# The scale of v of two batches as a sum on ScalarE instead of a maximum on VectorE, with a new table of turns

## The chip, the cores and the metric

One core of one Trainium2 chip. The time is that of the device for one execution, in microseconds. One execution of the kernel before was also recorded by the hardware profiler; all rows here are from it.

## The reference

Attention with random features (8 batches, 8 heads, 576 tokens, 64 wide, 128 features), then a feed-forward layer over the 4608 tokens, all in float32:

```python
def phi(x):                                   # x is q or k, scaled by 64 ** -0.25
    proj = np.einsum('bhsd,md->bhsm', x, omega)
    h = proj - np.sum(x * x, axis=-1, keepdims=True) / 2.0
    h = h - np.max(h, axis=-1, keepdims=True)
    return np.exp(h) / np.sqrt(m)
q_p, k_p = phi(q_s), phi(k_s)
kv = np.einsum('bhsm,bhsd->bhmd', k_p, v)
z = np.sum(k_p, axis=2)
num = np.einsum('bhsm,bhmd->bhsd', q_p, kv)
den = np.einsum('bhsm,bhm->bhs', q_p, z)[..., None] + 1e-06
x = (num / den) transposed to (4608, 512)
h = x @ w_in                                  # 512 to 2048
out = np.maximum(0.01 * h, h) @ w_out         # 2048 to 512
```

w_in and w_out come as 64-bit floats (8 MB each) and are turned into 32-bit words on the chip.

## The kernel before

Most matmuls run in float16, three for each product: a number is split into a high and a low half, and high by high, high by low and low by high are added. The first key batches (0 and 1) and the first query block run in float32 instead (`Whole`). Splitting is done by `high` (L412, L414 on VectorE, L416 on ScalarE) and `low_` (L422, VectorE or GpSimd).

The work goes over nine blocks of 512 tokens. For each pair of heads (hp) of a block, q is projected (L721 in float32, L657 in float16), its features are made on VectorE and ScalarE, turned (L912, or a transposing DMA), multiplied with kv (the numerators, L941 or L934 to L936) and divided (L951 to L954), which gives x. x is split and turned by a transposing DMA (L869) and goes through the feed-forward layer: up products (L1307 for the first three blocks, L1217 with seven products of half blocks after that), down products (L1331, at the end L1141). The low parts of the rows between them are L422 into `fix_big`, sums of half blocks are L983.

Keys come by batch: projection, features, and the sums with v (L824). Before that v of a batch gets a scale (`values`): a power of two made from one number for each partition. For that number VectorE reduces each of two halves of v (128x1280) to the largest absolute value (L759) and takes the larger of both (L762); `power_of_two` spreads it by a matmul (L447) and makes the power on VectorE (L451 to L456). v times that power is L416 on ScalarE. What the power was is taken out again in `row_scale`. The weights are read in eight pieces each (L516, L518), turned into float32 words (L531 to L554), summed for a scale (L544) and split (L578, L416, L422).

Every operation is recorded with its possible engines, a cost and its buffers. `Plan.order` then places them one after the other, by a model of the engines: the ready operation with the smallest priority goes first, and it takes the engine that would finish it first. Three tables change that order by the operation's number: TURNS moves its priority, HELD lets a matmul of the feed-forward layer wait or go earlier, ONLY names its engine. Tile buffers of a kind are handed out in the same order, so the table also sets which buffer an operation gets. Where the model sees TensorE idle for over 0.4 us, `between` puts throwaway matmuls (`busy`, L1382) that keep its clock up. All DMAs are issued by one queue (SP) in the order found.

The lines of the order's rule that the tables enter:

```python
o.prio -= 1e-4 * (o.tail - TURNS.get(o.number, 0.0))
t += SLACK["PE"] * o.slack + HELD.get(o.number, 0.0)
e = min([ONLY[o.number]] if o.number in ONLY else o.ways, key=...)
```

Of the kernel before, what the change touches and what calls it, by code (L numbers as in the profile page):

```python
# [1442 lines left out]
```

## Time and profile before

| | |
|---|---|
| median of 3 runs | 930.81 us (929.64 to 931.83) |
| profiled execution | 930.82 us, span 929.0 us |
| TensorE busy (PE) | 910.3 us, 98% |
| VectorE busy (DVE) | 737.3 us, 79% |
| ScalarE busy (ACT) | 561.1 us, 60% |
| GpSimd busy (POOL) | 374.4 us, 40% |
| mean granted clock of TensorE | 0.996 |

The span runs from the first to the last instruction. Busy times are sums of instructions; a busy TensorE includes the throwaway matmuls.

### The profile page before, as it was taken

What the parts mean: (1) busy time and instruction counts of PE and PEld (TensorE: products, weight loads), DVE (VectorE), ACT (ScalarE), POOL (GpSimd) and SP (SyncE); (2) the same over time, 40 slices, a digit from 0 to 9 for tenths busy, and PEclk for the clock granted to TensorE, in tenths of its full rate; (3) what the DMA queues carried; (4) which work ended last, traced back from release to release, by engine and by line L of the source; (5) the groups of instructions that cost most, each with busy time, mean ns of one, the idle gap of its engine ahead of it and who ended that gap; (6) DMA issues with size and microseconds to landing.
All of it is one profiled execution on the core that took longest, in us unless ns stands there. A gap on an engine that the chain in (4) does not pass through costs nothing.

```text
span 929.0 us, 20977 instructions
## 1 busy us (share of the span) xinstructions
PE 910.3 (98%) x8519; PEld 607.6 (65%) x8519; DVE 737.3 (79%) x1311; ACT 561.1 (60%) x867; POOL 374.4 (40%) x343
## 2 busy tenths in 40 slices
PE   7989999999999999999999999999999999999997
PEld 6887465545555445588558855885588558846886
DVE  7889988898888967888887889787889762476874
ACT  5888586756765556568647765575467545522551
POOL 2334443566615544236222532250226233664541
PEclk9999999999999999999999999999999999999999
DMA  9684538756477379678767876794688767721301
GB/s 355 256 273 133 129 102 170 177 134 171 77 187 149 84 183 232 154 192 206 188 126 178 223 161 147 185 210 91 136 197 206 140 126 176 165 58 60 100 1 46
DMA packets 257729, 145.92 MB, mean 157 GB/s; under 512 B 191328, under 2 KB 237152, under 8 KB 256608
## 3 DMA queue, kind: packets, MB, share of 16 engines
q1 hardware_dynamic: 257632, 144.58, 63.7%
q8 instruction: 66, 1.08, 0.5%
q14 instruction: 31, 0.25, 0.1%
HBM read 81.36 MB, written 16.78 MB: 106 GB/s over the span
## 4 chain that ended last, share of the span: by engine, by line
PE 84%; DMA 6%; DVE 4%; ACT 3%; POOL 1%; issue 1%; SPq 0%; DVEq 0%; ACTq 0%
PE fixps_ffn L1331 32%; PE fixps_ffn L1217 20%; PE fixps_ffn L1307 10%; PE attps_pj L657 5%; PE lateps_ffn L1331 3%; DMA fix_big<-w_in 3%; PE lateps_ffn L1217 3%; PE lateps_ffn L1141 2%; PE attps_mi L934 1%; DMA att_t<-att_z 1%; DMA att_qp<-att_ph 1%; POOL fix_wt L551 1%; PE fixps_ffn L1141 1%; PE attps_mi L824 1%; PE attps_mi L936 1%
## 5 line engine op out<-in xcount | busy, mean ns | idle before, releaser
L1331 PE MATMUL fixps_ffn<-fix_wt,fix_big 128*128 128x512 f16 x1392 | 313.2, 379 | 0.0
L1331 PEld LDWEIGHTS <-fix_big 128*128 128x128 f16 x1536 | 145.6, 98 | 166.6
L422 POOL TENSOR_TENSOR fix_big<-fix_row,fix_big 128x512 f16<-128x512 f32 x118 | 154.7, 1321 | 179.9 <-ACT fix_big L416 148.1
L1217 PEld LDWEIGHTS <-fix_wt 128*128 128x128 f16 x2016 | 194.9, 98 | 24.5
L1217 PE MATMUL fixps_ffn<-fix_xt,fix_wt 128*128 128x256 f16 x1800 | 204.3, 273 | 0.0
L1307 PE MATMUL fixps_ffn<-fix_xt,fix_wt 128*128 128x512 f16 x576 | 129.3, 379 | 0.0
L1307 PEld LDWEIGHTS <-fix_wt 128*128 128x128 f16 x576 | 54.7, 98 | 62.5
L676 ACT ACTIVATE att_p<-att_p,shift 128x1024 f32<-128x1024 f32 (+1 forms) x68 | 69.8, 1029 | 34.9 <-DVE att_p L673 34.7
L664 DVE TENSOR_REDUCE att_st<-attps_pj 128x8 f32<-128x1024 f32 x68 | 72.6, 1075 | 17.3 <-PE attps_pj L657 17.2
L422 DVE TENSOR_TENSOR att_ph<-att_p,att_ph 128x1024 f16<-128x1024 f32 x56 | 75.4, 1353 | 6.8 <-ACT att_ph L416 6.5
L416 ACT ACTIVATE fix_big<-fix_row 128x512 f16<-128x512 f32 x124 | 75.4, 624 | 8.4 <-DVE fix_row L983 5.3
L673 DVE SCALAR_TENSOR_TENSOR att_p<-attps_pj,att_sc,att_st 128x1024 f32<-128x1024 f32 x68 | 76.7, 1132 | 0.2
L1232 DVE TENSOR_TENSOR fix_row<-fix_row,fixps_ffn 128x512 f32<-128x512 f32 x64 | 43.8, 684 | 38.8 <-PE fixps_ffn L1217 20.7
L422 POOL TENSOR_TENSOR fix_xn<-fix_x,fix_xn 128x512 f16<-128x512 f32 (+1 forms) x28 | 31.8, 1134 | 90.4 <-ACT fix_xn L416 84.7
L617 ACT ACTIVATE att_z<-att_nat 128x512 f32<-128x512 f32 (+1 forms) x56 | 36.2, 647 | 43.6 <-DMA att_t<-att_z 35.0
L1240 ACT ACTIVATE fix_row<-fix_row 128x512 f32<-128x512 f32 x70 | 43.5, 624 | 18.3 <-DVE fix_row L1232 17.8
L657 PEld LDWEIGHTS <-att_t 64*128 64x128 f16 x1416 | 39.7, 94 | 19.1 <-issue 15.2
L416 ACT ACTIVATE att_ph<-att_p 128x1024 f16<-128x1024 f32 x48 | 50.4, 1049 | 3.0 <-PE attps_mi L824 1.6
L657 PE MATMUL attps_pj<-om,att_t 64*128 64x128 f16 x1416 | 50.3, 217 | 1.8 <-DMA att_t<-att_z 1.6
L416 ACT ACTIVATE fix_row<-fixps_ffn 128x512 f32<-128x512 f32 x47 | 27.8, 594 | 32.8 <-PE fixps_ffn L1217 29.3
L641 DVE SCALAR_TENSOR_TENSOR att_z<-att_nat,att_sc,att_z 128x512 f16<-128x512 f32 (+1 forms) x52 | 45.8, 881 | 2.2 <-ACT att_z L416 1.9
L416 ACT ACTIVATE fix_row<-fixps_ffn,fix_s 128x512 f32<-128x512 f32 x26 | 17.8, 683 | 49.3 <-PE fixps_ffn L1331 49.2
(202 smaller groups left out, 1645.2 us busy)
## 6 DMA issues: line engine op xcount, KB each, us to landing
fix_wt<-w1s SPq DMA_DIRECT2D x38, 512.0 KB, 4.9
fix_wt<-w1s SPq DMA_DIRECT2D x38, 384.0 KB, 3.7
att_v<-vn SPq DMA_DIRECT2D x16, 650.0 KB, 5.8
out<-fix_row SPq DMA_DIRECT2D x34, 256.0 KB, 2.3
fix_big<-w_in SPq DMA_DIRECT2D x8, 1024.0 KB, 11.2
fix_big<-w_out SPq DMA_DIRECT2D x8, 1024.0 KB, 6.5
att_nat<-qn SPq DMA_DIRECT2D x32, 256.0 KB, 3.0
w1s<-fix_y SPq DMA_DIRECT2D x32, 128.0 KB, 2.4
```

The source lines that it names most:

```text
L416: ("ACT", act(n, int(pointer)), lambda: nc.scalar.activation(dst(), src(), AF.Copy, scale=1.0 if scale is None else value()), False),
L422: return ways([(e, c, lambda g=g: g.tensor_tensor(dst(), a(), b(), op=ALU.subtract), True) for e, c, g in (("POOL", pool_(n), nc.gpsimd), ...
L641: op("DVE", stt(n) + 0.15, lambda: nc.vector.scalar_tensor_tensor(zl(), heads(), up(), zh(), op0=ALU.mult, op1=ALU.subtract), port=True, r ...
L657: nc.tensor.matmul(at(pj)[:, 512 * h + c * M:512 * h + (c + 1) * M], at(self.t)[r, 2 * (c0 + c) + x, :], om[r, w, :], start=(x + w == 0), ...
L664: op("DVE", dve(n * M), lambda: nc.vector.tensor_reduce(row(0), pv(), axis=AX.X, op=ALU.max), r=[pj], w=[st], prio=prio)
L673: op("DVE", dve(n * M), lambda: nc.vector.scalar_tensor_tensor(p(), pv(), down(), row(2).rearrange("p (g o) -> p g o", o=1).broadcast_to([ ...
L676: op("ACT", act(n * M, 1), lambda: nc.scalar.activation(flat(p()), flat(p()), AF.Exp, bias=shift), w=[p32], r=["ones"], prio=prio)
L1217: nc.tensor.matmul(o, unit(at(wb[c]), u)[:, wp, P * a:P * a + P], mixes[j, c][n][1](xp), start=(first and a == 0 and i == 0), stop=(a == 1 ...
L1232: op("DVE", dve(512), lambda: nc.vector.tensor_tensor(at(g), at(g), at(b), op=ALU.add), r=[b], w=[g], prio=top - 1.0)
L1240: op("ACT", act(512), lambda: nc.scalar.activation(at(g), at(src), AF.Prelu, scale=H_DOWN_D if finish else H_DOWN_S, alpha=0.01), r=[src], ...
L1307: nc.tensor.matmul(at(ph), wk[wp][:, c:c + P], xt[:, xp, :], start=(i == 0), stop=(i == 3 * KT - 1))
L1331: nc.tensor.matmul(at(po), part(f, gp)[:, t * P:(t + 1) * P], wf[wp], start=(n == 0 and f % 4 == 0 and gp == wp), stop=(n == 3 and f % 4 = ...
```

## The change

For batches 0 and 1 the two reduces of v on VectorE are replaced by two passes of ScalarE: the absolute value of a quarter of v, whose sum over the row (1280 numbers) the engine accumulates into the same two numbers. The values themselves go into a spare buffer of the kind z, which is not read. Everything behind it (the larger of the two, the power of two) is as it was; the power is another one and is taken out again like the first. Batches 2 to 7 keep the maximum. The three tables are replaced by new ones: TURNS has 2083 entries (214 before), HELD 220 (22) and ONLY 260 (109).

```diff
+V_ACT = (0, 1)
 READ_SUM = 0.2
 TURNS = {
-    17: -8162.408562, 19: 107.254804, 21: -271.649377, 24: -147.714435, 36: -50.284217, 51: 163.113317,
...
+    4: -247.528796, 5: -9365.02752, 6: -16958.431273, 7: -36741.43905, 8: -36505.728899, 9: -44080.908038,
...
         mx2, mx = one(f"mx2_v{b}", [P, 2]), one(f"mx_v{b}", [P, 1])
         for j in range(2):
-            op("DVE", dve(half * D), lambda j=j: nc.vector.tensor_reduce(mx2[:, j:j + 1],
-               at(raw)[:, j * half:(j + 1) * half, :D], axis=AX.XY, op=ALU.max, apply_absolute_value=True), r=[(raw, j)],
-               w=[f"mx2_v{b}{j}"], prio=prio)
+            x = lambda j=j: at(raw)[:, j * half:(j + 1) * half, :D]
+            if b not in V_ACT:
+                op("DVE", dve(half * D), lambda j=j, x=x: nc.vector.tensor_reduce(mx2[:, j:j + 1], x(), axis=AX.XY, op=ALU.max,
+                   apply_absolute_value=True), r=[(raw, j)], w=[f"mx2_v{b}{j}"], prio=prio)
+                continue
+            spare = buf("z")
+            op("ACT", act(half * D) + 0.25, lambda j=j, x=x, spare=spare: nc.scalar.activation(
+                at(spare).rearrange("p a b -> p (a b)").bitcast(BF16)[:, :half * D].rearrange("p (g d) -> p g d", d=D), x(),
+                AF.Abs, scale=0.25, accum_out=mx2[:, j:j + 1]), r=[(raw, j)], w=[spare, f"mx2_v{b}{j}"], prio=prio)
```

With the longer tables the code's lines move: L1307 is L1698 in the changed kernel, L954 is L1345, L516 is L901, L700 is L1085, L755 is L1140, L531 is L916, L416 is L801, L728 is L1113, L1382 is L1773.

The start of the program on the DMA queue. Before (kT, qT are keys and queries, omT is omega, vn is v, eye the identity):

```order
L700 DMA att_nat_159<-kT 128x640
L467 DMA fix_xt_98<-omT 128x256
L468 DMA ident<-eye 128x128
L516 DMA fix_big_88<-w_in 128x2048
L516 DMA fix_big_89<-w_in 128x2048
L516 DMA fix_big_90<-w_in 128x2048
L516 DMA fix_big_91<-w_in 128x2048
L755 DMA att_v_175<-vn 128x1300 x2
L700 DMA att_nat_160<-kT 128x640
L755 DMA att_v_176<-vn 128x1300 x2
```

Of the change:

```order
L901 DMA fix_big_88<-w_in 128x2048
L901 DMA fix_big_89<-w_in 128x2048
L901 DMA fix_big_90<-w_in 128x2048
L901 DMA fix_big_91<-w_in 128x2048
L1140 DMA att_v_175<-vn 128x1300
L1085 DMA att_nat_159<-kT 128x640
L1085 DMA att_nat_160<-kT 128x640
L1140 DMA att_v_175<-vn 128x1300
L852 DMA fix_xt_98<-omT 128x256
L853 DMA ident<-eye 128x128
```

Four pieces of w_in have moved ahead of keys, omega and identity.

VectorE where the scale of batch 0 is made (mx_v_128 holds the two numbers of its halves, mx_v_129 the larger). Before:

```order
L759 TENSOR_REDUCE mx_v_128<-att_v_175 128x1 x2
L536 SCALAR_TENSOR_TENSOR fix_wt_69<-fix_big_90,fix_wt_69 128x1024
L536 SCALAR_TENSOR_TENSOR fix_wt_71<-fix_big_91,fix_wt_71 128x1024
L762 TENSOR_REDUCE mx_v_129<-mx_v_128 128x1
L728 TENSOR_REDUCE att_st_179<-attps_pj_201 128x8
L451 TENSOR_REDUCE pow_v_130<-attps_mi_203 128x1
```

Of the change:

```order
L921 SCALAR_TENSOR_TENSOR fix_wt_71<-fix_big_91,fix_wt_71 128x1024
L864 TENSOR_SCALAR fix_xt_98<-fix_xt_98 128x256
L865 TENSOR_REDUCE mx_om<-fix_xt_98 128x1
L1153 TENSOR_REDUCE mx_v_129<-mx_v_128 128x1
L836 TENSOR_REDUCE pow_om<-attps_mi_203 128x1
```

The reduces of v are gone from there, and the scale of omega, which had been made before the first piece of w_in, is now made behind the fourth.

ScalarE at the end of the first query block (mx_v_135 belongs to batch 1, fix_xn to the split of x). Of the change:

```order
L801 ACTIVATE fix_xn_86<-fix_x_84 128x512
L934 ACTIVATE fix_wt_79<-fix_big_88 128x1024
L1150 ACTIVATE att_z_161,mx_v_135<-att_v_176 128x1280
L1150 ACTIVATE att_z_162,mx_v_135<-att_v_176 128x1280
L1086 ACTIVATE att_z_161<-att_nat_159 128x512
L1086 ACTIVATE att_z_162<-att_nat_160 128x512
L801 ACTIVATE fix_kv_82<-fix_kv_81 128x260
L801 ACTIVATE fix_xn_87<-fix_x_84 128x512
```

The two passes over v of batch 1 stand between the copies of x of the third and of the fourth pair of heads, where there was nothing of v.

## Rows read from the trace of the kernel before

**Rows 1.** Busy time of each engine in two stretches, cut at the start of the first up product (PE, PEld, DVE, ACT, POOL: us busy and instructions; then granted clock, share of the DMA engines, GB/s).

```profile
0.00:89.32 89.32, 79.14 (x848) 70.66 (x849) 76.11 (x124) 67.63 (x83) 27.31 (x22) 0.96 0.71 251
89.32:929.00 839.68, 831.12 (x7674) 536.95 (x7671) 661.19 (x1188) 493.43 (x786) 347.06 (x322) 1.00 0.64 147
```

**Rows 2.** Timeline of TensorE: the last numerators of the first query block, throwaway matmuls, the first up product, and the last matmuls of the program (start us, us, engine, line, operation).

```profile
81.23 1.10 PE L941 MATMUL attps_mi<-fix_kv,att_qp 128*128 128x65 f32 x8
85.06 4.42 PE L1382 MATMUL fixps_ffn<-ident 128*128 128x256 f16 x39
89.32 2.75 PE L1307 MATMUL fixps_ffn<-fix_xt,fix_wt 128*128 128x512 f16 x12
...
917.73 6.71 PE L1141 MATMUL lateps_ffn<-fix_wt,fix_big 128*128 128x256 f16 x60
```

**Rows 3.** What TensorE waited for, longest in total first (us in total, times, longest).

```profile
...
PE fixps_ffn L1141 <- DVE fix_big L422: 1.6, 1, 1.6
PE attps_pj L657 <- DMA att_t<-att_z: 1.6, 1, 1.6
```

**Rows 4.** Busy time of each engine from the start to the end of the eighth L954, in three stretches, and their sum (columns as in rows 1).

```profile
0.00:9.60 9.60, 4.56 (x38) 4.33 (x40) 3.62 (x17) 2.45 (x3) 0.20 (x4) 1.00 0.77 268
9.60:45.00 35.40, 33.57 (x399) 29.87 (x397) 32.73 (x43) 27.41 (x32) 10.66 (x10) 1.00 0.78 311
45.00:83.67 38.67, 35.47 (x362) 31.73 (x362) 34.14 (x56) 32.11 (x44) 13.23 (x7) 0.91 0.65 210
sum 83.67, PE 73.60 PEld 65.93 DVE 70.50 ACT 61.98 POOL 24.09; mean PE 24.53 PEld 21.98 DVE 23.50 ACT 20.66 POOL 8.03
```

**Rows 5.** Groups of VectorE instructions by line and shape (count, busy us and mean ns of one, then idle time before them).

```profile
L759 DVE TENSOR_REDUCE mx_v<-att_v 128x1 f32<-128x1280 f32 x16 | 23.5, 1479 | 1.7 <-DMA att_v<-vn 1.7
L422 DVE TENSOR_TENSOR fix_big<-fix_row,fix_big 128x512 f16<-128x512 f32 x23 | 20.1, 876 | 1.5 <-ACT fix_big L416 1.4
L730 DVE TENSOR_TENSOR att_ph<-attps_pj,att_st 128x1024 f32<-128x1024 f32 x12 | 14.6, 1218 | 0.8 <-DMA att_qp<-att_ph 0.8
L728 DVE TENSOR_REDUCE att_st<-attps_pj 128x8 f32<-128x1024 f32 x12 | 14.6, 1214 | 1.8 <-PE attps_pj L721 1.8
L533 DVE TENSOR_SCALAR fix_wt<-fix_wt 128x1024 uint32<-128x1024 uint32 x16 | 13.5, 851 | 2.5 <-ACT fix_wt L531 1.5 <-issue 0.9
L412 DVE CAST att_ph<-att_p 128x1024 f16<-128x1024 f32 x8 | 6.4, 806 | 0.2 <-ACT att_p L676 0.2
L412 DVE CAST fix_xn<-fix_y 128x512 f16<-128x512 f32 x4 | 2.1, 513 | 0.0
L414 DVE TENSOR_SCALAR fix_row<-fixps_ffn,fix_s 128x512 f32<-128x512 f32 x2 | 1.5, 752 | 3.5 <-PE fixps_ffn L1331 3.5
L422 DVE TENSOR_TENSOR fix_kv<-fix_kv,fix_kv 128x260 f16<-128x260 f32 x2 | 0.8, 416 | 0.0
```

**Rows 6.** Timeline of VectorE: the division behind a numerator, with the idle time before it and what ended that (in brackets), and the eighth L954.

```profile
73.67 0.16 DVE L951 TENSOR_SCALAR att_r<-attps_mi 128x4 f32<-128x4 f32 x1 [1.15 <-PE attps_mi L941]
...
83.24 0.42 DVE L954 TENSOR_TENSOR fix_x<-attps_mi,att_r 128x256 f32<-128x256 f32 x1
```

**Rows 7.** Timelines of the queue (SPq), ScalarE and GpSimd: issues at the start, the first instructions that waited for pieces of w_in and for the second block of keys, and the high and low part of the fourth pair of heads.

```profile
0.74 0.41 SPq L700 DMA_DIRECT2D att_nat<-kT  x1
...
2.13 1.85 SPq L516 DMA_DIRECT2D fix_big<-w_in  x4
...
9.17 1.13 ACT L531 ACTIVATE fix_wt<-fix_big 128x1024 f32<-128x1024 f32 x1 [4.50 <-DMA fix_big<-w_in]
...
16.59 1.18 ACT L531 ACTIVATE fix_wt<-fix_big 128x1024 f32<-128x1024 f32 x1 [0.30 <-DMA fix_big<-w_in]
...
21.38 0.74 ACT L701 ACTIVATE att_z<-att_nat 128x640 f32<-128x640 f32 x1 [0.92 <-DMA att_nat<-kT]
...
84.50 0.62 ACT L416 ACTIVATE fix_xn<-fix_x 128x512 f16<-128x512 f32 x1
...
85.20 1.21 POOL L422 TENSOR_TENSOR fix_xn<-fix_x,fix_xn 128x512 f16<-128x512 f32 x1 [3.23 <-ACT fix_xn L416]
```

**Rows 8.** Groups of ScalarE instructions by line and shape, and busy time of each engine from 70 to 85 us (columns as in rows 5 and 1).

```profile
L416 ACT ACTIVATE att_v<-att_v,pow_v 128x1280 f32<-128x1280 f32 x16 | 21.3, 1350 | 0.0
L617 ACT ACTIVATION_READ_ACCUMULATOR att_z<-att_nat 128x1 f32 x56 | 10.5, 188 | 0.0
L701 ACT ACT_TABLE_LOAD x1 | 1.3, 1283 | 0.7 <-PEq L1436 0.7
...
70.00:85.00 15.00, 14.29 (x138) 12.39 (x137) 13.74 (x22) 10.85 (x17) 4.37 (x2) 0.91 0.36 104
```

**Rows 9.** Timeline of TensorE: the first and the last of the sixteen rows of four matmuls of two projections in f32 (L721) that stand back to back.

```profile
59.01 0.49 PE L721 MATMUL attps_pj<-fix_xt,att_nat 64*128 64x128 f32 x4
...
62.46 0.39 PE L721 MATMUL attps_pj<-fix_xt,att_z 64*128 64x128 f32 x4
```

**Rows 10.** Busy time of each engine from 590 to 690 us (columns as in rows 1).

```profile
590.00:690.00 100.00, 99.56 (x1004) 70.40 (x1003) 81.78 (x156) 62.43 (x103) 25.91 (x26) 1.00 0.71 159
```

**Rows 11.** Timelines of VectorE and of GpSimd near the end: two sums of half blocks (L983) on VectorE, and what GpSimd ran at the time of the first.

```profile
902.26 1.65 DVE L983 TENSOR_TENSOR fix_row<-fix_row,fix_row 128x512 f32<-128x512 f32 x1
...
909.23 0.68 DVE L983 TENSOR_TENSOR late_row<-late_row,fix_row 128x512 f32<-128x512 f32 x1
...
902.09 2.83 POOL L422 TENSOR_TENSOR fix_big<-fix_row,fix_big 128x512 f16<-128x512 f32 x2 [3.98 <-DVE fix_big L412]
```

More of the change, by code (lines that the diff above doesn't have):

```diff
@@ L113 @@
-    1365: "DVE", 1420: "DVE", 1485: "DVE", 1593: "DVE", 1597: "DVE", 1612: "DVE", 1646: "DVE", 1649: "DVE",
-    1656: "DVE", 1664: "DVE", 1672: "DVE", 1693: "DVE", 1699: "DVE", 1741: "DVE", 1916: "DVE", 1926: "DVE",
-    1927: "DVE", 1934: "DVE", 1953: "DVE", 1956: "DVE", 1957: "DVE", 1972: "DVE", 1992: "DVE", 2008: "DVE",
-    2011: "DVE", 2025: "DVE", 2044: "DVE", 2048: "DVE", 2053: "DVE", 2174: "DVE", 2184: "DVE", 2188: "DVE",
-    2195: "DVE", 2198: "DVE", 2204: "DVE", 2226: "DVE", 2258: "DVE", 2304: "DVE", 2307: "DVE", 2311: "DVE",
@@ L118 @@
-    2314: "DVE", 2365: "DVE", 2375: "DVE", 2470: "DVE", 2537: "DVE", 2540: "DVE", 2541: "DVE", 2547: "DVE",
-    2569: "DVE", 2627: "DVE", 2629: "DVE", 2737: "DVE", 2740: "DVE", 2752: "DVE", 2759: "DVE", 2765: "DVE",
-    2824: "DVE", 2884: "DVE", 2897: "DVE", 2913: "DVE", 2966: "DVE", 2976: "POOL", 2977: "DVE", 3007: "POOL",
-    3014: "POOL", 3027: "DVE", 3030: "ACT", 3036: "POOL", 3046: "DVE", 3059: "POOL", 3082: "DVE", 3092: "DVE",
-    3095: "POOL", 3113: "DVE",
+    77: "DVE", 102: "DVE", 210: "DVE", 313: "DVE", 314: "DVE", 325: "DVE", 333: "DVE", 334: "DVE", 342: "DVE",
@@ new lines @@
+    346: "POOL", 350: "DVE", 357: "DVE", 376: "DVE", 460: "DVE", 465: "DVE", 479: "DVE", 483: "DVE", 486: "DVE",
+    490: "DVE", 492: "DVE", 497: "DVE", 499: "DVE", 502: "DVE", 503: "DVE", 505: "DVE", 538: "DVE", 564: "DVE",
+    565: "DVE", 661: "DVE", 688: "DVE", 712: "DVE", 717: "DVE", 723: "DVE", 762: "DVE", 802: "ACT", 898: "DVE",
+    929: "DVE", 953: "DVE", 961: "DVE", 965: "DVE", 976: "DVE", 977: "DVE", 984: "DVE", 985: "DVE", 1001: "DVE",
+    1004: "DVE", 1005: "DVE", 1009: "DVE", 1019: "ACT", 1025: "DVE", 1084: "DVE", 1134: "DVE", 1136: "DVE",
@@ new lines @@
+    1138: "DVE", 1139: "DVE", 1140: "DVE", 1141: "DVE", 1143: "DVE", 1204: "DVE", 1253: "DVE", 1276: "DVE",
+    1306: "DVE", 1315: "DVE", 1330: "DVE", 1340: "DVE", 1353: "DVE", 1359: "DVE", 1371: "DVE", 1485: "DVE",
+    1492: "DVE", 1495: "DVE", 1596: "DVE", 1597: "DVE", 1600: "DVE", 1631: "DVE", 1640: "DVE", 1659: "DVE",
+    1665: "DVE", 1670: "DVE", 1679: "DVE", 1694: "DVE", 1701: "DVE", 1707: "DVE", 1711: "DVE", 1712: "DVE",
+    1785: "DVE", 1843: "DVE", 1869: "DVE", 1877: "DVE", 1880: "DVE", 1930: "DVE", 1933: "DVE", 1934: "DVE",
@@ new lines @@
+    1935: "DVE", 1936: "DVE", 1940: "DVE", 1948: "DVE", 1950: "DVE", 1966: "DVE", 1972: "DVE", 1976: "DVE",
+    1982: "DVE", 1996: "DVE", 2000: "DVE", 2001: "DVE", 2006: "DVE", 2025: "DVE", 2034: "DVE", 2037: "DVE",
+    2044: "DVE", 2047: "DVE", 2052: "DVE", 2053: "DVE", 2087: "DVE", 2098: "DVE", 2120: "DVE", 2128: "DVE",
+    2152: "DVE", 2187: "DVE", 2188: "DVE", 2190: "DVE", 2191: "DVE", 2192: "DVE", 2193: "DVE", 2194: "DVE",
+    2204: "DVE", 2212: "DVE", 2241: "DVE", 2290: "DVE", 2293: "DVE", 2300: "DVE", 2303: "DVE", 2304: "DVE",
@@ new lines @@
+    2340: "DVE", 2359: "DVE", 2370: "DVE", 2372: "DVE", 2379: "DVE", 2393: "DVE", 2407: "DVE", 2408: "DVE",
+    2412: "POOL", 2416: "ACT", 2429: "DVE", 2435: "DVE", 2441: "DVE", 2455: "DVE", 2477: "DVE", 2516: "DVE",
+    2534: "DVE", 2535: "DVE", 2537: "DVE", 2538: "DVE", 2547: "DVE", 2580: "DVE", 2594: "ACT", 2626: "DVE",
+    2629: "ACT", 2630: "DVE", 2633: "DVE", 2634: "DVE", 2635: "DVE", 2636: "DVE", 2637: "DVE", 2639: "ACT",
+    2640: "DVE", 2643: "DVE", 2648: "POOL", 2656: "DVE", 2666: "DVE", 2667: "DVE", 2671: "ACT", 2672: "POOL",
@@ new lines @@
+    2676: "ACT", 2677: "DVE", 2682: "DVE", 2685: "DVE", 2686: "POOL", 2692: "DVE", 2695: "DVE", 2696: "POOL",
+    2705: "ACT", 2706: "DVE", 2708: "DVE", 2714: "ACT", 2715: "DVE", 2730: "POOL", 2735: "POOL", 2740: "ACT",
+    2743: "DVE", 2747: "DVE", 2753: "DVE", 2759: "DVE", 2771: "DVE", 2813: "ACT", 2823: "ACT", 2824: "POOL",
+    2826: "DVE", 2827: "DVE", 2829: "DVE", 2830: "POOL", 2831: "DVE", 2833: "DVE", 2834: "DVE", 2865: "DVE",
+    2873: "DVE", 2891: "DVE", 2893: "DVE", 2894: "DVE", 2896: "DVE", 2897: "DVE", 2928: "DVE", 2930: "DVE",
@@ new lines @@
+    2938: "DVE", 2959: "DVE", 2964: "POOL", 2967: "POOL", 2969: "DVE", 2982: "DVE", 2983: "POOL", 2998: "DVE",
+    3002: "DVE", 3006: "POOL", 3009: "POOL", 3014: "POOL", 3016: "ACT", 3017: "DVE", 3024: "ACT", 3035: "ACT",
+    3036: "POOL", 3046: "ACT", 3047: "POOL", 3049: "ACT", 3050: "POOL", 3055: "POOL", 3062: "DVE", 3064: "DVE",
+    3065: "POOL", 3067: "POOL", 3077: "DVE", 3091: "DVE", 3093: "POOL", 3095: "DVE", 3096: "DVE", 3102: "POOL",
+    3103: "DVE", 3106: "POOL", 3108: "POOL", 3110: "POOL", 3112: "POOL", 3114: "DVE", 3116: "POOL", 3117: "DVE",
@@ L123 @@
+    3124: "DVE", 3133: "DVE", 3140: "DVE", 3141: "DVE", 3149: "DVE", 3156: "DVE", 3164: "DVE",
 }
```

4 lines of the change are left out of this document (removed), and 444 rows, old and new, of tables (HELD, TURNS).

## The prediction

> **What bounds the kernel now.** The two stretches of [rows 1] come first, cut at the start of the first up product (L1307) at 89.32 us [rows 2]. From there to the end TensorE is busy for 831.1 of 839.7 us, so that part is the matmuls themselves. In the 89.3 us ahead of it TensorE only serves a chain that others pace. The order of the changed program has the same matmuls on both sides of the first up product; only the throwaway matmuls (L1382, all ahead of it) go from 233 to 205. So the time is the start of the first up product, plus 831.1 us that neither order changes, plus whatever TensorE waits behind it, now 8.6 us. The waits of TensorE [rows 3] list two longer ones there, 1.6 us for the transposed z (at about 110 us) and 1.6 us for VectorE's low part of a half block (at 908.8 us); 4.6 us more are the drain from the last matmul, 924.4, to the end of the span [rows 2].
>
> The stretch ahead of the first up product is paced by VectorE. Its last instruction that matters there is the eighth L954 (the second half of x of the fourth pair of heads), which ends at 83.67 us [rows 6]; up to there it works 70.5 us and idles 13.2 [rows 4]: 6.0 in the first 9.6 us, 2.7 to 45 and 4.5 to 83.7. One wait of the last part is 1.15 us for TensorE's numerators [rows 6]. From 83.67 it takes 5.65 us more: high part on ScalarE, low part on GpSimd, transposing DMA [rows 2, 7].
>
> **VectorE's list.** I count what stands in VectorE's queue ahead of the eighth L954, 115 instructions before and 114 now. Gone are the four reduces of batches 0 and 1 (but the two of batch 2 now stand ahead of it, so a net two), two L728, one L730 and one L533. At the durations of [rows 5]: 2 x 1.48 + 2 x 1.21 + 1.22 + 0.85 = 7.45 us. New are a cast of a weight piece (nearest row 0.81), a cast of x (0.51), and two small ones of kv (0.42 each; one of them has the row, the other I take alike): 2.16 us; one more maximum of two numbers I leave out. Net -5.3, so 65.2 us of work.
>
> **What ScalarE pays.** An Abs pass over 128x1280 with a sum is not in the trace. The nearest row is the L416 copy of v of the same shape, 1.35 us, plus the read of the accumulator, 0.19 us [rows 8]: 1.54 us each, 6.2 us in all. Free is not excluded by any row for the first two (ScalarE waits there for transfers, [rows 7]); the upper bound is the sum. The order has one table load before and one now, so none is added to the 1.28 us of [rows 8]. The passes of batch 0 take the place of waiting. Those of batch 1 stand ahead of the copy of x of the fourth pair; ScalarE is idle for 4.15 us between 70 and 85 us [rows 8], which covers them; without that cover they cost 3.1 us there.
>
> **The transfers move.** The queue now begins with four pieces of w_in, and the keys, omega and the identity, which were first, come behind them. The first row of the queue issues at 0.74 us; the first piece of w_in was issued at 2.13 and had landed at 9.17 [rows 7], 7.0 us later, so it should now land at 7.8 and VectorE start on it at 8.9, after ScalarE's 1.13. The fourth piece had landed at 16.59, 7.4 us behind the first, so it is there at 15.2. Omega stands behind 6.3 MB; the second block of keys stood behind 6.4 MB and landed at 21.4, so omega is there at about 21.2, where before its chain was over by 8.3. VectorE's idle time now: 8.2 us to the first piece; to about 25.7 us 1.5 for the pace of the pieces, 1.9 for omega, 0.9 inside the omega chain (as its wait for L447 now) and 0.4 for the first projection; then 2.0 to 45 us (2.7 from 9.6 to 45 now, nearly all of it behind 20). Behind 45 us it was 4.5. In the new order the weights are converted earlier and the queries' projections stand ahead of the sums, so I take 1.5, with 0 and 4.5 as ends. Sum 16.4 us, 3.2 more than now.
>
> So the eighth L954 ends at 65.2 + 16.4 = 81.6 us, 2.1 us earlier. Behind it the data need the high part, 0.62, the low part, 1.21, and 2.9 from its end at 86.4 to the up product at 89.3 [rows 2, 7]: 4.7 us. TensorE still has 64 projections of batch 1 (3.85 us from 59.01 to 62.85, [rows 9]), 22 throwaway matmuls at 0.109 (39 in 4.24, [rows 2]) and one group of sums (0.2) between the last numerator and the up product, 6.45 us, counted from 1.3 us ahead of the end of L954: 5.1. So the first up product starts at 86.7, **-2.6 us**.
>
> **Behind the first up product.** The projection that waited 1.6 us for its transposed z had seven up products (2.6 us each) between the start and itself; now it has eight. I take half the wait, -0.8, with 0 and -1.6 as ends. The wait at 908.8 I leave as it is (0 to -1.65). The new table also moves work onto VectorE for the rest of the run: 48 more L422, 36 more casts (L412), 16 more L414, four fewer L983; at 0.88, 0.51 and 0.75 us [rows 5], and 0.9 for the last (between the 0.68 and 1.65 of [rows 11]), that is 42 + 18 + 12 - 4, less 5.9 for the four reduces: +62 us. GpSimd has 44 instructions fewer, ScalarE 43. VectorE goes from 737 to 799 us, of some 926. The cover is its idle time, 178 us of the 839.7 [rows 1]. The densest added stretch has ten more L422 and ten more L412, 13.9 us on the 81.8 of 100 between 590 and 690 us [rows 10]: 96, still under. I price it at nothing, with +7 us as the other end (third rival).
>
> **Sum.** 930.82 (this execution, span 929.0 and 1.82 around it; the median of the runs shown is 930.81) - 2.6 - 0.8 = **927.4 us**. No other time is taken from the table.
>
> **One row against a rule.** Beside GpSimd's additions of 1.6 us the same L983 takes VectorE 1.65 us, and 0.68 alone [rows 11]: about 1 us lost for each overlap. The Trainium skill (SBUF — State Buffer, Who interferes with whom) says that a VectorE instruction with both inputs in SBUF and a GpSimd instruction that reads SBUF exclude each other, and that the later one blocks until the first is done. The trace agrees. By that rule the 48 moved L422 are exposed to lock-outs that they did not have on GpSimd, and at 1 us each that would be another 48 us, 847 of some 926; but GpSimd also has 44 instructions fewer to lock with. The sum goes by the mean rows, in which the overlaps of now are contained.
>
> **Rivals.**
> *The front costs more than it gives* (0.17). Keys and omega come 15 us later. If the transfers of the first two query blocks, behind 12.2 MB, land at 38 us and not 35, the chain of the queries starts 3 us later, and VectorE's idle time behind 45 us stays at 4.5. For it: behind 6.4 MB the second keys landed at 21.4 [rows 7], so 12.2 MB at the same pace are there at 36 and not earlier. Against it: VectorE has conversions to do until then. First up product at 89 to 90 us, total 930.
>
> *All of it is gained* (0.16). VectorE never idles behind 45 us (-1.5), and both waits of TensorE go (-0.8 and -1.65 more): 923.5. For it: the list alone is 5 us shorter, and the new order has 28 throwaway matmuls fewer, 3.0 us of TensorE. Against it: three engines must arrive together at the numerators, as they did not in [rows 6].
>
> *VectorE locks out in the down products* (0.15), the other side. The moved L422 sit between a finished half block and the products that read it. One place like that waits 1.65 us now [rows 3, 11]. If the added instructions make such a wait at each of four more places in the last six blocks, that is +6.6, total 934 (927.4 + 6.6). It decides from the second such wait on, which eats the 3.4.
>
> That the change doesn't do what it says I exclude: the order has no reduce for batches 0 and 1.
>
> **How the numbers follow.** The likeliest case (0.49) has its own range of 924.5 to 930 from the ends of the idle time and the two waits; I give 0.40 of it to faster and 0.09 to same. A measurement tells about 0.2%, 1.9 us, from no change. The front rival gives 0.13 to same, 0.04 to slower; the full gain 0.16 to faster; the lock-out 0.14 to slower, 0.01 to same; 0.03 is left for what I don't see (0.01 each). That makes 0.57, 0.24 and 0.19. The range runs from just under the full gain, 922.5, to 932, between the front rival and the lock-out.
>
> **What would show it.** In the changed profile: first w_in conversion on ScalarE near 7.8 us; Abs rows of 1.3 to 1.55 us, no second table load; VectorE busy 65 us up to the eighth L954 (there L1345), which ends near 82; the first up product (L1698) near 87 (86 to 90) with as much TensorE time behind it; no 1.6 us wait at z; VectorE 780 to 800 us in all; TensorE's waits behind the first up product at most 9 us. The prediction is wrong if the first up product is later than 89, if TensorE's idle time behind it grows past 11 us, or if the granted clock falls there.

## The result: 939.6 us, slower by 0.9%

The changed kernel takes 939.62 us (median of 4 runs, 938.11 to 940.42) against 931.32 us before: ratio 1.0092, 95% interval 1.0078 to 1.0107. The forecast was 927.4 us, with a range of 922.5 to 932.

The profiled execution has a span of 937.1 us, 8.1 more than before. Busy time of each engine, cut at the start of the first up product (L1698), with the columns of [rows 1]:

```profile
0.00:91.33 91.33, 71.34 (x820) 63.57 (x821) 72.00 (x119) 66.61 (x82) 28.26 (x22) 1.00 0.69 244
91.33:937.10 845.77, 833.63 (x7674) 535.79 (x7671) 695.63 (x1280) 471.57 (x747) 294.40 (x278) 1.00 0.62 146
```

The first up product starts 2.0 us later than before, and the part behind it is 6.1 us longer: 845.8 for 839.7. What TensorE waited for in the whole program, to be read against [rows 3]:

```profile
PE fixps_ffn L929 <- DVE fix_wt L921: 10.9, 2, 8.9
PE attps_pj L1773 <- DMA ident<-eye: 9.5, 1, 9.5
PE attps_pj L1042 <- DMA att_t<-att_z: 2.2, 1, 2.2
PE attps_mi L1327 <- DMA att_qp<-att_ph: 1.9, 2, 1.3
PE fixps_ffn L1698 <- ACT fix_row L1705: 0.9, 1, 0.9
```

The sum of the 8.1:

- 2.0: the later first up product (91.33 against 89.32).
- 3.6: more idle time of TensorE behind it, 12.1 against 8.6 by the rows of both kernels. Nearly all of it is in longer waits, 7.4 us in sum against 3.7. By the timeline of TensorE they are 2.06 us at the sums of w_out (L929, at 115.8 us) and 0.88 at the up product next to it, 0.26 and 1.33 for a low part of kv and a transposed q near 182 and 190 us, 0.62 at 452, and 2.20 for a transposed z at 727. Before they were the two of 1.6 in [rows 3] and one of 0.44.
- 2.5: more busy time for the same matmuls. 1.7 of it is one place, two up products behind the wait at 115.8, below; the rest is spread.
- The drain is as before (4.6 from the last matmul).

**The front.** Timeline of TensorE in the changed kernel, from its first work to the spread of omega (L832):

```profile
8.87 0.37 PE L929 MATMUL fixps_ffn<-ones,fix_wt 128*128 128x1 bf16 x8 [8.87 <-DVE fix_wt L921]
18.69 5.79 PE L1773 MATMUL attps_pj<-ident 128*128 128x256 f16 x35 [9.45 <-DMA ident<-eye]
24.32 0.34 PE L929 MATMUL fixps_ffn<-ones,fix_wt 128*128 128x1 bf16 x8
...
27.66 0.34 PE L929 MATMUL fixps_ffn<-ones,fix_wt 128*128 128x1 bf16 x8
...
28.08 0.39 PE L832 MATMUL attps_mi<-ident,mx_om 128*128 128x128 f32 x2
```

VectorE's timeline over the same time, with the idle time before an instruction in brackets (L865 is the maximum of omega, L836 the first use of the spread):

```profile
20.05 0.42 DVE L865 TENSOR_REDUCE mx_om<-fix_xt 128x1 f32<-128x256 f32 x1
20.39 0.14 DVE L1153 TENSOR_REDUCE mx_v<-mx_v 128x1 f32<-128x2 f32 x1
28.51 0.29 DVE L836 TENSOR_REDUCE pow_om<-attps_mi 128x1 f32<-128x128 f32 x1 [7.98 <-PE attps_mi L832]
```

And the DMA queue's issues, the first pieces of w_in and the identity:

```profile
0.74 2.24 SPq L901 DMA_DIRECT2D fix_big<-w_in  x4
...
8.16 0.33 SPq L853 DMA_DIRECT2D ident<-eye  x1
```

VectorE had the maximum of omega at 20.5. It then stood still for 7.98 us. The spread of that number is an instruction of TensorE, and in its queue 64 throwaway matmuls stand ahead of it, between the sums of w_in. Those read the identity. The identity is now the tenth row of the queue, issued at 8.16, and was there at 18.69: TensorE waited 9.45 us for it, and only then began to do what had been put into the gap of 9 to 20 us. The end of the front, on VectorE (the eighth division) and on TensorE (the first up product):

```profile
85.46 0.42 DVE L1345 TENSOR_TENSOR fix_x<-attps_mi,att_r 128x256 f32<-128x256 f32 x1
```

```profile
91.33 1.89 PE L1698 MATMUL fixps_ffn<-fix_xt,fix_wt 128*128 128x512 f16 x8
```

The eighth division ends at 85.88 (83.67 before, [rows 6]), and 5.45 us behind it the first up product starts.

**The pause at 114 us.** Timeline of TensorE there, and busy times behind the pause, with the granted clock in the column behind the five engines:

```profile
104.88 5.34 PE L1698 MATMUL fixps_ffn<-fix_xt,fix_wt 128*128 128x512 f16 x24
...
115.84 0.35 PE L929 MATMUL fixps_ffn<-ones,fix_wt 128*128 128x1 bf16 x8 [2.06 <-DVE fix_wt L921]
117.07 7.03 PE L1698 MATMUL fixps_ffn<-fix_xt,fix_wt 128*128 128x512 f16 x24 [0.88 <-ACT fix_row L1705]
```

```profile
117.00:120.00 3.00, 2.93 (x9) 1.10 (x9) 3.00 (x5) 1.14 (x3) 0.00 (x0) 0.66 0.02 5
120.00:123.00 3.00, 3.00 (x12) 1.28 (x11) 2.97 (x5) 1.42 (x3) 2.18 (x2) 0.77 0.01 3
```

The sums of a piece of w_out wait for VectorE, which is busy without a gap from 99 to 120 us. Behind the pause two up products take 7.03 us, where two others take 5.34. The granted clock (as a share of full speed) is 0.66 and 0.77 there: part of the time at the lower of its two levels, 1.2 GHz, after TensorE had stood still for 2.06 and 0.88 us with one short row between.

**ScalarE's passes.** Groups of its instructions by line and shape, and its one table load:

```profile
L1150 ACT ACTIVATE att_z<-att_v 128x1280 bf16<-128x1280 f32 x4 | 5.1, 1278 | 0.4 <-DMA att_v<-vn 0.4
...
L1150 ACT ACTIVATION_READ_ACCUMULATOR att_z<-att_v 128x1 f32 x4 | 0.8, 206 | 0.0
...
L916 ACT ACT_TABLE_LOAD x1 | 1.3, 1283 | 0.7 <-PEq L1827 0.7
```

### The profile page after: what moved, and what is told of

Same layout as the page of the kernel before. It is cut to its first block, busy times and chain, and to the rows that moved or that the text cites. A ratio compares the mean times of both kernels' runs of the same rounds, so it can differ in the third digit from the quotient of the medians.

```text
span 937.1 us, 20905 instructions
## 1 busy us (share of the span) xinstructions
PE 905.0 (97%) x8491; PEld 599.4 (64%) x8491; DVE 767.6 (82%) x1398; ACT 538.2 (57%) x828; POOL 322.7 (34%) x299
## 3 DMA queue, kind: packets, MB, share of 16 engines
q8 instruction: 66, 1.08, 0.5%
## 4 chain that ended last, share of the span: by engine, by line
PE 82%; DVE 8%; DMA 5%; ACT 3%; issue 2%; SPq 0%; DVEq 0%; ACTq 0%
PE fixps_ffn L1722 28%; PE fixps_ffn L1608 20%; PE fixps_ffn L1698 11%; PE attps_pj L1042 4%; PE lateps_ffn L1722 3%; PE lateps_ffn L1532 2%; PE lateps_ffn L1608 2%; PE attps_pj L1106 2%; DMA att_t<-att_z 2%; DMA att_qp<-att_ph 1%; ACT fix_wt L801 1%; PE attps_mi L1325 1%; DMA ident<-eye 1%; PE attps_pj L1773 1%; PE fixps_ffn L1532 1%
## 5 line engine op out<-in xcount | busy, mean ns | idle before, releaser
L1608 PE MATMUL fixps_ffn<-fix_xt,fix_wt 128*128 128x256 f16 x1836 | 209.3, 273 | 0.0
L807 POOL TENSOR_TENSOR fix_big<-fix_row,fix_big 128x512 f16<-128x512 f32 x91 | 118.9, 1312 | 228.4 <-ACT fix_big L801 174.9
L1698 PE MATMUL fixps_ffn<-fix_xt,fix_wt 128*128 128x512 f16 x576 | 130.3, 383 | 0.9 <-ACT fix_row L1705 0.9
L1698 PEld LDWEIGHTS <-fix_wt 128*128 128x128 f16 x576 | 55.3, 99 | 65.0 <-issue 3.1
L807 POOL TENSOR_TENSOR fix_xn<-fix_x,fix_xn 128x512 f16<-128x512 f32 (+1 forms) x29 | 31.4, 1084 | 146.8 <-ACT fix_xn L801 105.1
L807 DVE TENSOR_TENSOR att_ph<-att_p,att_ph 128x1024 f16<-128x1024 f32 x56 | 72.0, 1289 | 9.0 <-ACT att_ph L801 8.8
L801 ACT ACTIVATE fix_big<-fix_row 128x512 f16<-128x512 f32 x110 | 67.2, 623 | 14.5 <-DVE fix_row L1374 9.9
L801 ACT ACTIVATE att_ph<-att_p 128x1024 f16<-128x1024 f32 x50 | 52.0, 1048 | 2.0 <-PE attps_mi L1229 1.2
L801 ACT ACTIVATE fix_row<-fixps_ffn 128x512 f32<-128x512 f32 x53 | 31.3, 592 | 30.1 <-PE fixps_ffn L1608 27.9
L1026 DVE SCALAR_TENSOR_TENSOR att_z<-att_nat,att_sc,att_z 128x512 f16<-128x512 f32 (+1 forms) x52 | 47.7, 918 | 0.5 <-ACT att_z L801 0.3
L1705 ACT ACTIVATE fix_row<-fixps_ffn 128x512 f32<-128x512 f32 x48 | 28.3, 591 | 33.6 <-PE fixps_ffn L1698 32.2
```

What stands on the lines that cost most here:

```text
L801: ("ACT", act(n, int(pointer)), lambda: nc.scalar.activation(dst(), src(), AF.Copy, scale=1.0 if scale is None else value()), False),
L807: return ways([(e, c, lambda g=g: g.tensor_tensor(dst(), a(), b(), op=ALU.subtract), True) for e, c, g in (("POOL", pool_(n), nc.gpsimd), ...
L1026: op("DVE", stt(n) + 0.15, lambda: nc.vector.scalar_tensor_tensor(zl(), heads(), up(), zh(), op0=ALU.mult, op1=ALU.subtract), port=True, r ...
L1608: nc.tensor.matmul(o, unit(at(wb[c]), u)[:, wp, P * a:P * a + P], mixes[j, c][n][1](xp), start=(first and a == 0 and i == 0), stop=(a == 1 ...
L1698: nc.tensor.matmul(at(ph), wk[wp][:, c:c + P], xt[:, xp, :], start=(i == 0), stop=(i == 3 * KT - 1))
```

## The experiments

Medians of 4 to 11 runs. The ratio is that to the kernel before on the same chip; the runs were made on several chips, so small differences are read from the ratios, and a difference of two of them is uncertain by some 1.5 to 2.5 us, as the intervals show. Lines of the kernels behind an edit move by a few (the throwaway matmuls, L1773, are L1774 to L1781). In the diffs, ... stands for lines left out.

| run | time, us | ratio (95% interval) | first up product in the profile, us |
|---|---|---|---|
| the changed kernel | 939.62 | 1.0092 (1.0078 to 1.0107) | 91.33 |
| no front fill | 937.77 | 1.0069 (1.0052 to 1.0086) | 86.11 |
| identity first | 932.75 | 1.0019 (1.0007 to 1.0030) | 84.84 |
| old tables with the edit | 951.51 | 1.0221 (1.0192 to 1.0250) | 96.67 |
| maximum in the new order | 943.92 | 1.0137 (1.0118 to 1.0156) | 97.14 |
| identity first, maxima behind x | 936.37 | 1.0056 (1.0042 to 1.0070) | 86.66 |
| identity first, maxima behind w_out | 935.87 | 1.0058 (1.0043 to 1.0072) | 84.52 |
| identity first, pause filled | 929.24 | 0.9986 (0.9978 to 0.9995) | 84.88 |
| pause filled, identity late | 936.97 | 1.0064 (1.0042 to 1.0087) | 91.27 |

**No throwaway matmuls ahead of the spread of omega.** Operation 4 is the spread.

```diff
     fill = between(order)
+    front = order.index(next(o for o in order if o.number == 4))
+    fill = {o: x for o, x in fill.items() if order.index(o) > front}
```

> The changed kernel without the 64 throwaway matmuls that stand in TensorE's queue ahead of the spread of omega (L832); nothing else moves. Theory A (they are what holds the front: they read the identity, which lands at 18.7 us now, and VectorE then idles 8.0 us until the spread at 28.0): the spread runs at about 20.6 us, the first projections run slower by some 2 us because TensorE has done nothing before, VectorE's first maximum of projections starts near 25 instead of 31.0, the first up product at 85 to 87 instead of 91.3, the time 933 to 935, or 929 to 930 if the wait and the low clock at 114 to 122 us go as well. Theory B (the front is paced by VectorE's list and by transfers, the stall at 20 us is cover): first up product at 90 to 91.5, the time 938 to 940.

The spread runs at 20.92 and the first up product at 86.11, as theory A said, by the timeline of TensorE in this run:

```profile
20.92 0.79 PE L832 MATMUL attps_mi<-ident,mx_om 128*128 128x128 f32 x2 [0.28 <-DVE mx_v L1153]
```

```profile
86.11 4.26 PE L1698 MATMUL fixps_ffn<-fix_xt,fix_wt 128*128 128x512 f16 x19
```

The identity is as late here as in the changed kernel (10.5 us from issue to landing in both), so it is the throwaway matmuls in front of the spread that turned its lateness into 7 us of idle VectorE.

The time agrees less well. The median, 937.77, fell by 1.9 us only and lies above theory A's 933 to 935, just under theory B's 938 to 940. The profiled run is the fastest of the six (935.01 us; the slowest took 939.25), and it has a mean granted clock of 1.000, where the other five have 0.996 to 0.998: their clock fell, at places that are not recorded. In the profiled run the pause behind the up products is there again (2.50 and 0.87 us) but the clock did not fall; TensorE's waits behind the first up product are 9.2 us in sum, 1.8 more than in the changed kernel. And the price of leaving the throwaway matmuls out shows: the first rows of projections behind the spread took 0.64 us here and 0.39 in the next run, whose first up product is 1.3 us earlier.

**The identity first.** Operation 1 is the load of the identity; every other instruction keeps its place.

```diff
     fill = between(order)
+    order.sort(key=lambda o: o.number != 1)
```

> The changed kernel with one DMA moved: the identity (64 KB) is issued first on the queue, ahead of the pieces of w_in; all other instructions keep their order, the throwaway matmuls too. Theory A: the throwaway matmuls run while the pieces are converted, the spread of omega runs at 20.5 to 21 us, projections at the warm pace, VectorE's idle time there falls from 8.0 to about 1, the first up product starts 5 to 7.5 us earlier, at 84 to 86, the time 932 to 934 (928 to 929 if the stall at 114 to 122 us goes too). Theory B: no change, 938 to 940.

Timeline of TensorE in this run: the spread, the first up product, and the pause:

```profile
21.17 0.49 PE L832 MATMUL attps_mi<-ident,mx_om 128*128 128x128 f32 x2
```

```profile
84.84 7.93 PE L1698 MATMUL fixps_ffn<-fix_xt,fix_wt 128*128 128x512 f16 x36
...
109.38 0.35 PE L929 MATMUL fixps_ffn<-ones,fix_wt 128*128 128x1 bf16 x8 [2.08 <-DVE fix_wt L921]
110.61 7.03 PE L1698 MATMUL fixps_ffn<-fix_xt,fix_wt 128*128 128x512 f16 x24 [0.87 <-ACT fix_row L1705]
```

One DMA of 64 KB issued 7.4 us earlier is worth 6.9 us of the median (939.62 to 932.75; ratio 1.0092 to 1.0019) and 6.5 at the first up product. Theory A holds, by two ways of taking the same obstacle away. VectorE's wait for the spread falls from 7.98 to 0.52 us, and the first up product and the time are where theory A had them. But the pause at the sums of w_out comes with it, 2.08 and 0.87 us, with the same 7.03 us for two up products: the part behind the first up product stays at 846.2. That second loss does not hang on the first.

**The edit with the old tables.** The three tables of the kernel before, whole, in the changed code (HELD and ONLY likewise).

```diff
 TURNS = {
-    4: -247.528796, 5: -9365.02752, 6: -16958.431273, 7: -36741.43905, 8: -36505.728899, 9: -44080.908038,
...
+    17: -8162.408562, 19: 107.254804, 21: -271.649377, 24: -147.714435, 36: -50.284217, 51: 163.113317,
...
```

> The edit alone: the changed code (sums on ScalarE for batches 0 and 1) with the three tables of the kernel before. The rule makes another order from them since costs differ. If the edit is worth what it takes from VectorE's list ahead of the eighth division (four reduces of 1.48, 5.9 us, of which two of batch 2 may move in again), 925 to 931. If the tables count more than the edit, the order that comes out is untuned and slower than before: 932 to 950.

951.51: the second expectation, and 1.5 us above its range. The first up product is at 96.67, and behind it TensorE waits at many places where there were three. Its waits in this run, longest in total first (L658 is a projection, L545 the sums of the weights, L1224 and L1314 up products):

```profile
PE attps_pj L658 <- DMA att_t<-att_z: 5.2, 7, 1.4
...
PE fixps_ffn L545 <- DVE fix_wt L537: 4.0, 4, 2.4
PE fixps_ffn L1224 <- ACT fix_row L417: 2.8, 3, 1.1
PE fixps_ffn L1314 <- DMA fix_xt<-fix_xn: 1.7, 1, 1.7
```

The rule orders by modelled costs, and a few costs moved from VectorE to ScalarE give a wholly different order under numbers that were found for another. What the edit alone is worth can't be read from this run. It says that the tables hold for one set of costs.

**The maximum again, in the new order.** The four passes run on VectorE at the places that the new order gives them.

```diff
-            op("ACT", act(half * D) + 0.25, lambda j=j, x=x, spare=spare: nc.scalar.activation(
-                at(spare).rearrange("p a b -> p (a b)").bitcast(BF16)[:, :half * D].rearrange("p (g d) -> p g d", d=D), x(),
-                AF.Abs, scale=0.25, accum_out=mx2[:, j:j + 1]), r=[(raw, j)], w=[spare, f"mx2_v{b}{j}"], prio=prio)
+            op("ACT", act(half * D) + 0.25, lambda j=j, x=x: nc.vector.tensor_reduce(
+                mx2[:, j:j + 1], x(), axis=AX.XY, op=ALU.max, apply_absolute_value=True), r=[(raw, j)], w=[spare, f"mx2_v{b}{j}"], prio=prio)
```

> The changed kernel's order with the edit undone: the four passes over v of batches 0 and 1 are VectorE's maximum again, each at its place in the program; the tables and the rest of the order are those of the change. Theory A (VectorE idles 8 us behind 20.5 us): the two of batch 0 are swallowed there, the two of batch 1 cost up to 3.0 us: first up product at 91 to 94.5, the time 939 to 943. If the edit's effect is nil or ScalarE's passes cost as much: 939. If the tables are the whole loss and the edit is worth its 5.9 us: 944 to 946.

VectorE's wait for the spread of omega in this run:

```profile
28.32 0.29 DVE L836 TENSOR_REDUCE pow_om<-attps_mi 128x1 f32<-128x128 f32 x1 [5.02 <-PE attps_mi L832]
```

TensorE's numerators behind the passes of batch 1, the first up product, and busy times with the granted clock (0.66, as above the column behind the engines) from 85 to 95 us:

```profile
86.51 1.97 PE L1331 MATMUL attps_mi<-fix_kv,att_qp 128*128 128x65 f32 x8 [3.06 <-DVE fix_x L1344]
...
97.14 3.19 PE L1697 MATMUL fixps_ffn<-fix_xt,fix_wt 128*128 128x512 f16 x14
```

```profile
85.00:95.00 10.00, 8.49 (x77) 8.20 (x78) 7.14 (x13) 2.77 (x4) 1.43 (x2) 0.66 0.41 109
```

As theory A had it, the two passes of batch 0 cost nothing: VectorE waits 5.02 us instead of 7.98, and goes on at 28.3 as before. The two of batch 1 are late in front of the numerators (TensorE waits 3.06 us for the division; the eight matmuls behind take 1.97 us, where the last group of the changed kernel took 1.11, at the lower clock). In all 4.3 us: in this order the edit is worth that much, the clock's fall included, so the loss is not its own. The whole of it comes with the new order, which with the maximum is 1.37% above the kernel before. Theory A's bounds did not hold, though: the time is 0.9 us above its 943, next to the 944 to 946 of the third expectation, and the first up product 2.6 us later than its 94.5; the lower clock behind the wait had not been counted.

**Two maxima of batch 2 moved back.** Both on top of the identity first; 745, 746 are the maxima and 747 the larger of both, 139 the eighth division, 272 and 545 instructions of VectorE near 117 and 120 us.

```diff
...
+    order.remove(number[746])
+    order.insert(order.index(number[139]) + 1, number[746])
+    order.remove(number[745])
+    order.insert(order.index(number[746]) + 1, number[745])
+    order.remove(number[747])
+    order.insert(order.index(number[745]) + 1, number[747])
```

In the second run:

```diff
...
+    order.remove(number[746])
+    order.insert(order.index(number[272]) + 1, number[746])
+    order.remove(number[745])
+    order.insert(order.index(number[545]) + 1, number[745])
+    order.remove(number[747])
+    order.insert(order.index(number[745]) + 1, number[747])
```

> On top of the run with the identity first (932.75 us, first up product 84.8): VectorE's two maxima of batch 2 and the larger of both, which stand between the last divisions (73.9 to 77.3 us), are moved right behind the eighth division; nothing else. They are still ahead of the last five conversions of w_out. Theory C (the start of the first up product sets the time, TensorE's work behind it is fixed): it starts up to 2.9 us earlier, at 82 to 83, and the time falls with it to 930. Theory D (VectorE's whole list up to the last conversion of w_out, at about 115 us, sets the pace; an earlier start only makes TensorE wait longer at the sums of w_out): the first up product starts earlier, the wait at the sums grows from 2.1 to 4 to 5 us, and the time stays at 932 to 933.5.

> The same two maxima of batch 2 moved further, behind the conversions of w_out: one to where VectorE idles 1.2 us at 117, one to 121 us. Theory D: the list is 2.9 us shorter up to the last conversion, the first up product starts at 82 to 83 and the wait at the sums stays as it is (2 us), so the time falls by the whole 2.9, to 929.5 to 930.5. Theory C says the same 930 here and differs in the run before. If neither: 932.75 as without the move.

Both expectations missed: slower by 3.6 and 3.1 us than with the identity first alone (3.4 and 3.6 by the ratios), and theories C and D are not told apart, because the eighth division did not come earlier. It ended at 79.5 in both, with 2.9 us less ahead of it (79.4 without the move). Timeline of TensorE in the second run:

```profile
73.22 1.08 PE L1332 MATMUL attps_mi<-fix_kv,att_qp 128*128 128x65 f32 x8 [0.29 <-DVE fix_x L1345]
...
74.47 2.89 PE L1781 MATMUL attps_pj<-ident 128*128 128x256 f16 x25
77.20 1.00 PE L1332 MATMUL attps_mi<-fix_kv,att_qp 128*128 128x65 f32 x8
```

Its VectorE and, below, its GpSimd at that time:

```profile
75.38 0.42 DVE L1345 TENSOR_TENSOR fix_x<-attps_mi,att_r 128x256 f32<-128x256 f32 x1 [0.68 <-POOL fix_xn L807]
75.72 3.03 DVE L807 TENSOR_TENSOR fix_wt<-fix_wt,fix_wt 128x1024 f16<-128x1024 f32 x1
78.68 0.15 DVE L1342 TENSOR_SCALAR att_r<-attps_mi 128x4 f32<-128x4 f32 x1
```

```profile
75.31 2.37 POOL L936 TENSOR_TENSOR fix_wt<-fix_wt,fix_wt 128x1024 f32<-128x1024 f32 x1
```

VectorE in the run with the identity first alone, one of the maxima and the same L807, and the same addition of GpSimd there:

```profile
75.58 1.46 DVE L1146 TENSOR_REDUCE mx_v<-att_v 128x1 f32<-128x1280 f32 x1
...
77.34 1.22 DVE L807 TENSOR_TENSOR fix_wt<-fix_wt,fix_wt 128x1024 f16<-128x1024 f32 x1
```

```profile
75.11 2.37 POOL L936 TENSOR_TENSOR fix_wt<-fix_wt,fix_wt 128x1024 f32<-128x1024 f32 x1
```

VectorE's own list took most of the freed time. The seventh L1345 waits 0.68 us for GpSimd. The low part of a weight (L807, two inputs in SBUF) moved into the slot of the maxima, beside an addition of GpSimd: 3.03 us, where it took 1.22 without the move. The two come to 2.5 us, and the last division (L1342 to L1345) starts right behind L807, at 78.68, without a wait. The maximum had run beside the same addition, in 1.46 us. The Trainium skill (SBUF — State Buffer, Who interferes with whom) says that a VectorE instruction with two inputs in SBUF and a GpSimd instruction that reads SBUF block each other, the second to issue until the first is done, and that a reduce never contends; these rows agree: GpSimd's addition ends at 77.68, and L807, started at 75.72, ends 1.07 us behind that. Close behind stands a second limit. Between the last two groups of numerators are 25 throwaway matmuls, 2.9 us that TensorE does whether or not anything waits, so these numerators end at 78.2; without the longer L807 the last division would have started there, 0.5 us earlier.

In the first run the maxima also held up a sum of w_out ahead of the first up product (a wait of 1.93 us, first up product at 86.66). In the second run TensorE's waits behind 120 us grew, and its granted clock was at 0.70 and 0.66 in two more stretches (180 to 185 and 725 to 730 us). Part of the loss of both runs goes with the clock: the mean granted clock of their six executions is 0.996 and 0.995 on average, against 0.997 with the identity first alone, and both profiled ones, at 0.995 and 0.993, are the slowest of their six.

**The pause filled.** On top of the identity first, 14 and 5 throwaway matmuls ahead of the sums of w_out (265) and of the next up product (327), into the bank of a later projection (568).

```diff
...
+    fill[number[265]] = number[568].bufs[-1], 14
+    fill[number[327]] = number[568].bufs[-1], 5
```

> On top of the run with the identity first: 14 throwaway matmuls (1.5 us) ahead of the sums of w_out for which TensorE waits 2.1 us at 107 to 109 us, and 5 (0.5 us) ahead of the up product that waits 0.9 us behind it, into a bank that is free; nothing else. If the granted clock falls behind this pause because TensorE stood still (it took 7.03 us for two up products, 5.34 elsewhere), the two take 5.3 again, and the time falls by 1.7 us where that clock fell, to 931. If the clock's fall has another cause, or the throwaway matmuls hold up the products as much: 932.75 to 933.5.

Timeline of TensorE in this run, at the pause:

```profile
107.28 1.70 PE L1777 MATMUL attps_pj<-ident 128*128 128x256 f16 x14
109.41 0.35 PE L929 MATMUL fixps_ffn<-ones,fix_wt 128*128 128x1 bf16 x8 [0.42 <-DVE fix_wt L921]
109.62 0.70 PE L1777 MATMUL attps_pj<-ident 128*128 128x256 f16 x5
110.63 5.34 PE L1698 MATMUL fixps_ffn<-fix_xt,fix_wt 128*128 128x512 f16 x24 [0.31 <-ACT fix_row L1705]
```

The up product behind the pause starts at the same time as without them (110.63 and 110.61), and two take 5.34 us again. So the throwaway matmuls won back the 1.7 us that the clock had cost. The median fell by more, 3.5 us (3.1 by the ratios), to 929.24. In the profiles the waits further on are shorter too (2.7 us after 4.7), which was not expected and is not explained here. The clock is steadier as well: all 11 runs have a mean of 0.999 or 1.000, where with the identity first alone it went from 0.995 to 1.000, and the one of those at 1.000 took 930.20. This version is the fastest of all, 0.14% below the kernel before (interval 0.05 to 0.22%), which is less than the 0.2% that the prediction had called a change.

**The pause filled, the identity late.** The same two lines on the changed kernel, without the move of the identity.

> The changed kernel as it is, the identity late, with only the 14 and 5 throwaway matmuls in the pause at 114 to 117 us (as in the run that had both, 929.24, against 932.75 with the identity first alone). If the two losses are separate, the first up product stays at 91.3, the two up products behind the pause take 5.3 instead of 7.0, and the time is 939.62 - 3.5 = 936.1 (935.5 to 937). If the pause's cost hangs on the start of the first up product, or the 3.5 came from elsewhere: 938.5 to 939.6.

Timeline of TensorE in this run: the first up product where it was in the changed kernel, and the two behind the pause:

```profile
91.27 7.93 PE L1698 MATMUL fixps_ffn<-fix_xt,fix_wt 128*128 128x512 f16 x36
...
117.02 5.34 PE L1698 MATMUL fixps_ffn<-fix_xt,fix_wt 128*128 128x512 f16 x24 [0.30 <-ACT fix_row L1705]
```

936.97, at the upper end of what was expected for separate losses. So the two stand side by side: the identity 6.9 us with the pause empty and 7.7 with it filled (6.8 and 7.3 by the ratios), the pause 2.7 with the identity late and 3.5 with it first (2.6 and 3.1), which the intervals do not tell apart.

## Why the prediction was wrong, step by step

The profiled run is 11.5 us above the forecast: 4.6 at the first up product (91.33 for 86.7) and 6.9 behind it (845.8 for 838.9).

**The step that failed first: what the omega chain waits for.** The prediction gave VectorE 1.9 us of idle time for omega and "0.9 inside the omega chain (as its wait for L447 now)". The transfer was no worse than forecast: omega there at 21.2 by the prediction, used at 19.74 without a wait and its maximum done at 20.5 in the trace. The 0.9 was 7.98. It was taken from a program in which the identity came third and nothing stood ahead of the spread on TensorE. The issue of the identity and VectorE's wait there, in the kernel before:

```profile
1.67 0.42 SPq L468 DMA_DIRECT2D ident<-eye  x1
```

```profile
5.88 0.29 DVE L451 TENSOR_REDUCE pow_om<-attps_mi 128x1 f32<-128x128 f32 x1 [0.89 <-PE attps_mi L447]
```

The prediction said itself that the identity moves behind four pieces of w_in, and it counted the throwaway matmuls, but as TensorE time only (28 fewer, 3.0 us); that they read the identity and stand in a queue in front of an instruction that VectorE waits for was left out. Moving the one DMA is worth 6.9 us.

**The rest of the front erred both ways, and by luck hid part of the first error.** The first conversion of w_in on ScalarE ran at 5.71, not 7.8. VectorE's work up to the eighth division is 66.8 us against 65.2 (its nine conversions L918 took 1.08 us each, where the row had 0.85). Its idle time is 19.1 against 16.4, and without the wait for the spread 11.1 against 15.5. So 7.1 us too little in one term showed as 4.6 at the first up product. With the identity first the idle time is 12.6, and the division ends at 79.39 against the forecast 81.6. From there to the first up product it took 5.45 us in both, forecast 5.1. The edit's own price was right: 1.28 and 0.21 us for a pass, 1.48 against 1.54, no second table load. The two passes of batch 1 cost nothing at the copy of x behind them: ScalarE stood idle for 0.66 us ahead of it, at 85.96, just behind the division.

**The second step that failed: "831.1 us that neither order changes" and the wait at 110.** The matmuls are the same, but 2.5 us of their busy time are new, 1.7 of them from the clock behind one pause. The wait for the transposed z at 110 did go from its place, wholly and not by half. But the sums of w_out had come to stand there instead, and wait longer; another z waits 2.20 at 727. The prediction had looked at this place for one transfer, not for what VectorE has to deliver there, although VectorE is busy all the time in it. For this term it had -0.8; it was +6.1. Filling the pause showed that the clock is a part of it (5.34 for 7.03 us).

**What was priced at nothing was nothing.** No wait of the changed kernel stands in the down products; the lock-out rival didn't happen, and the wait at 908.8 is gone. VectorE is busy for 767.6 us, not 799. By groups of the same shape, the added instructions are some 56 us (the four reduces taken off), but the means of the groups fell, which makes some 19 less (the low parts of 128x1024, 1.28 us against 1.34; the additions of 128x512, 0.72 against 0.76); the rest is overlap of instructions that follow each other. That the 44 instructions fewer on GpSimd behind the first up product are the reason, because there is less to lock with, is likely and not shown. The prediction had mentioned that and not priced it.

**Of its signs,** it had named three by which it would be wrong: a first up product later than 89 (91.33), more than 11 us of idle TensorE behind it (12.1), a fall of the granted clock there (0.66). All three came. The front rival had the right place and sign (0.17, 930 us), with another mechanism: the transfers of the queries, not the identity. Its sum does not come out either: at the pace that it names, 6.4 MB by 21.4 us, 12.2 MB would be there at some 40 us, not at 36. And where the prediction has GpSimd's additions beside the L983 of 1.65 us, [rows 11] show two low parts (L422).

What stays open: why the granted clock falls behind some pauses and in some executions, and not in others; why the waits at 180 to 190 and 727 us come with the new order and shrink when an earlier pause is filled, and whether the start of the first up product or VectorE's list sets the time up to 120 us.

## To carry to other kernels

When an order moves a small transfer back, list every instruction that reads it and every instruction queued behind those; a constant that filler work reads first can hold up the whole program, because what stands behind the filler in the engine's queue waits too. A gap in a planner's model is not a gap on the chip: filler should be bound to operands that are surely there. And a wait of the kernel before is a number for the queue in which it was measured, so where the order changes, read what stands ahead in the new queue before taking it over.
